# Softmax sums in 16 matmuls a step instead of 32, with the halves of each sum added by VectorE, and one side unit moved ahead of the second scores

## Chip, cores and metric

The kernel runs on one core of a Trainium2 chip. The metric is the device time of one execution in microseconds (us). Before the change the median of three runs is 751.95 us (751.55 to 753.9).

## What is computed

Two branches over the same 2048 x 512 input x are mixed by a gate. Branch A is a recurrent attention with memory: the sequence is cut into 64 segments of 32 tokens, each segment attends to itself and to 8 memory tokens, and the first 8 rows of a segment's output are the memory of the next. Branch B is a layer norm with a two-layer MLP. Cut to what matters here:

```
for s in range(64):                                  # 64 segments, in order
    h = concat([mem, x[s*32:(s+1)*32]])              # 8 + 32 rows
    q, k, v = h @ Wq, h @ Wk, h @ Wv                 # 32 heads of 128
    scores = where(mask, q @ k.T * scale, -1e9)
    p = softmax(scores)                              # exp / sum of exp
    o = (p @ v) @ Wo
    mem = o[:8]                                      # needed by the next segment
    outs.append(o[8:])
out = g * concat(outs) + (1 - g) * mlp(layernorm(x)) # g = sigmoid(sum(x * gate_w))
```

Because the memory is carried, a segment can't begin before the memory rows of the one ahead are known.

## The kernel before, in words

A first part of some 80 us loads all weights into SBUF and runs most of the MLP. Then a Python loop writes out 64 steps, one per segment. The order of the instructions on every engine is the order of the program text; nothing is rescheduled.

**Packing.** A step works on 32 columns at once: the 8 memory rows and 24 of the 32 tokens; the other 8 tokens of a segment ("left") have had their projections made ahead, four segments at a time. TensorE runs mostly in four strips of 32 columns (`tile_position=(0, 32 * j)`), so four matmuls in a row work side by side and a group of four is the unit to count. The 32 heads stand as 8 groups (i) of 4 (j); the first four groups are half 0, the others half 1. Each half has its own PSUM bank of scores, `SbF` for half 0 and `U[0]` for half 1, 56 columns a group.

**A step, in TensorE's order.** Four projections of queries and keys (`qk_unit`, L128, into `U`), each cast by ScalarE (L133) and transposed by VectorE (L137). Then `scores(s, 0)` (L266 and L270), whose exponentials ScalarE writes to the tile `E` (L805). Five V units (`v_unit`, L147). The sums for half 0. `scores(s, 1)`, whose exponentials come in two pieces (L794): columns 40 to 55, which belong to the memory queries, first, then columns 0 to 39. Two V units, a side unit, the memory sums of half 1, the last V unit. Two units of other work, a side unit, the side sums of half 1. Then the attention product `av` (L290 with V, L295 with VP; half 0 first, then half 1), and the output projection (L159), whose memory rows go through `new_mem` (L746, cast by VectorE in L748) into the next step's input.

**Two kinds of sums.** The sums for the memory queries (`msum`, L796) are needed at once: `mnorm` takes their reciprocal on VectorE (L801) and multiplies the columns 40 to 55 of `E` by it (L802) before `av` reads them. `sums` (L273) makes them in two rows of four matmuls, main part (L277) and left part (L280), which add up in PSUM. The sums for the other 32 queries (`xsums`, L697) can come later, since their product is divided afterwards: L701 makes them with the exponentials as the stationary operand, in two rows of four again, into 8 columns `xs8` of `SbF`. `recip_x` takes their reciprocal (L712), sends it to DRAM (`r_dr`, L715) and back, broadcast to all partitions, as `Rb` (L718), on SP's DMA queue, with the loads of `hm` (L646) between. In the next step POOL multiplies by it (`x_norm`, L730).

**Side units.** `next(mlp)` issues four matmuls of 256 columns (L674) of the MLP that was put off for some tiles. They wait for nothing in the step and are put at places by hand. `racc` (L722) and `rmin` (L865) collect the reciprocals for a range test at the end; `mask_put` (L259) writes the mask, and zeros for the sums, into `SbF` or `U[0]`.

Of the kernel before, what the change touches and what calls it, by code (L numbers as in the profile page):

```python
# [28 lines left out]
def kernel(ctx, tc, A_x, A_mem0, A_Wq, A_Wk, A_Wv, A_Wo, A_seg_len, B_x, B_w1, B_b1, B_w2, B_b2, gate_w, out):  # L29
    nc = tc.nc  # L30
    P = 128
    _, S, Dm = A_x.shape
    H, Dh = A_Wq.shape[1], A_Wq.shape[2]
    M = A_mem0.shape[1]
# [10 lines left out]
    NG = H // 4  # L45
    NP = H // 2
    EW = 56
    RIDE = 32 - M
    LEFT = seg - RIDE
# [8 lines left out]
    dram = ctx.enter_context(tc.tile_pool(name="dram", bufs=1, space=DRAM))  # L58
# [22 lines left out]
    MkF = ep.tile([P, 4 * EW + NG + 2 * M], BF16)  # L81
# [169 lines left out]


    RS = ep.tile([P, 32], FP32)
    RP = [SbF[:, 288:320], RS[:]]


    def mask_put(i2):
        c = 4 * EW + (NG + 2 * M if i2 == 0 else 0)
        nc.vector.tensor_copy(out=(SbF, U[0])[i2][:, 0:c], in_=MkF[:, 0:c])  # L259

    def scores(s, i2):
        T, si = divmod(s, SPT)
        for i in range(4 * i2, 4 * i2 + 4):
            for j in range(4):
                h = 4 * i + j
                nc.tensor.matmul(Sb[i2][32 * j:32 * j + 32, i - 4 * i2, M:M + 40], lhsT=KT[:, h // 2, :, h % 2], rhs=QT[:, h // 2, :, h % 2],  # L266
                                 start=False, stop=True, skip_group_check=True, tile_position=(0, 32 * j))
        for j in range(4):
            a0 = 8 * i2 + j // 2
            nc.tensor.matmul(Sb[i2][32 * j:32 * j + 32].rearrange("p i (a b) -> p i a b", b=8)[:, :, 0:7:6, :],  # L270
                             lhsT=KL[T % 2][:, si, j // 2, i2].rearrange("p l a b -> p (l a) b")[:, :, j % 2],
                             rhs=QT[:, a0:a0 + 7:2, :, j % 2].rearrange("p a (x q) -> p a x q", q=8)[:, :, 0:5:4, :],
                             start=False, stop=True, skip_group_check=True, tile_position=(0, 32 * j))  # L273

    def sums(out, E, c_main, c_left, n, start):
        for j in range(4):
            nc.tensor.matmul(out[32 * j:32 * j + 32], lhsT=BO[:, 32 * j:32 * j + 32], rhs=E[:, :, c_main:c_main + n],  # L277
                             start=start, stop=False, skip_group_check=True, tile_position=(0, 32 * j))
        for j in range(4):
            nc.tensor.matmul(out[32 * j:32 * j + 32, :, 0:8], lhsT=BO[:, 32 * j:32 * j + 32], rhs=E[:, :, c_left:c_left + 8],  # L280
                             start=False, stop=True, skip_group_check=True, tile_position=(0, 32 * j))
# [315 lines left out]
    racc = lp.tile([P, NG * 40], FP32)  # L597
    rmin = lp.tile([P, NG * 40], FP32)
    tot = lp.tile([P, 4], FP32)
    good = lp.tile([P, 2], BF16)  # L600
# [89 lines left out]
    mlp = mlp_halves()  # L690
    XRs, Rbs = {}, {}

    xs8 = SbF[:, 4 * EW:4 * EW + NG]
    xs8z = SbF[:, 4 * EW + NG:4 * EW + NG + 2 * M]
    RW = 9 * NG

    def xsums(E, h):  # L697

        for c0, n in ((8, 32), (0, LEFT)):
            for c in range(4):  # L700
                nc.tensor.matmul(xs8[32 * c:32 * c + n, 4 * h:4 * h + 4], lhsT=E[:, 4 * h + c, c0:c0 + n], rhs=BO[:, 0:P:32],  # L701
                                 start=False, stop=True, skip_group_check=True, tile_position=(0, 32 * c))

    def x_raw(s):
        XR = cx.tile([P, 4, NG, 32], BF16, tag="XR", name="XR")
# [3 lines left out]

    def recip_x(s):  # L710
        R = Rs.pop(s)
        nc.vector.reciprocal(out=R[:, 8 * NG:RW], in_=xs8)  # L712

        Rb = cw.tile([P, P, NG], FP32, tag="Rb", bufs=1, name="Rb")
        nc.sync.dma_start(r_dr[s % 2][:], R[:, 8 * NG:RW])  # L715
        hm_load(owed[0])
        owed[0] = 0
        nc.sync.dma_start(Rb[:].rearrange("p r e -> p (r e)"), r_dr[s % 2][:].rearrange("r e -> (r e)").partition_broadcast(P))  # L718
        for i2 in (1, 0):
            nc.vector.tensor_copy(out=R[:, 32 * i2:32 * i2 + 32], in_=RP[i2])  # L720
        mask_put(0)
        nc.gpsimd.tensor_tensor(out=racc[:, 0:RW], in0=racc[:, 0:RW], in1=R[:, 0:RW], op=ALU.add)  # L722
        Rbs[s] = Rb

    def x_norm(s):
        T, si = divmod(s, SPT)
        XR, Rb = XRs.pop(s), Rbs.pop(s)[:].rearrange("p (c q) (h j) -> p h j c q", c=4, h=2)
        for out, o, a, b in ((UT[(s + 1) % 2], M, LEFT, 32), (UL[T % 2], LEFT * si, 0, LEFT)):
            for h in range(2):
                nc.gpsimd.tensor_tensor(out=out[:, :, 4 * h:4 * h + 4, o:o + b - a], in0=XR[:, :, 4 * h:4 * h + 4, a:b], in1=Rb[:, h, :, :, a:b], op=ALU.mult)  # L730

    def wo_pass(U_, cuts=(0, Dm), bk=W):
        for n in range(NW):
# [19 lines left out]
    for s in range(nseg):  # L753
        T, si = divmod(s, SPT)
# [6 lines left out]
        if s >= 1:  # L761
            x_norm(s - 1)
# [24 lines left out]
        E = cx.tile([P, NG, EW], BF16, tag="E", name="E")  # L787
        R = cx.tile([P, NG * 40], FP32, tag="R", name="R")
# [5 lines left out]
            nc.scalar.activation(out=E[:, 4 * i2:4 * i2 + 4, c], in_=Sb[i2][:, :, c], func=ACTF.Exp, scale=scale)  # L794

        def msum(i2):  # L796
            sums(U[1 + 2 * i2][:, 320:352].rearrange("p (i q) -> p i q", q=8), E[:, 4 * i2:4 * i2 + 4, :], 40, 48, 8, True)

        def mnorm(i2):
            r, e = RP[i2], E[:, 4 * i2:4 * i2 + 4, 40:56].rearrange("p i (a q) -> p i a q", q=8)  # L800
            nc.vector.reciprocal(out=r, in_=U[1 + 2 * i2][:, 320:352])  # L801
            nc.vector.tensor_tensor(out=e, in0=e, in1=r.rearrange("p (i q) -> p i q", q=8).unsqueeze(2).to_broadcast([P, 4, 2, 8]), op=ALU.mult)  # L802

        scores(s, 0)
# [94 lines left out]
    wl, c = wls.pop(T), cs.pop(T)  # L899
    o = cw.tile([P, Dm], BF16, tag="o", bufs=1, name="o")  # L900
# [159 lines left out]
```

## Time and profile before

| | us |
|---|---|
| median of three runs | 751.95 |
| the profiled execution | 755.67 |
| its span, first to last instruction | 753.8 |
| TensorE busy | 736.0 (98%) |
| ScalarE busy | 535.6 (71%) |
| VectorE busy | 399.5 (53%) |
| POOL busy | 274.2 (36%) |

The profile is of one execution. A row of a timeline gives the start in us from the span's start, the busy time, the engine, the line of the program, the operation, the tiles out<-in, their sizes and how many instructions are merged in it; in square brackets stands how long the engine was idle before and what ended that. A row of a group by shape has busy time, mean ns of one instruction, and idle time ahead. PE is TensorE's matmul, PEld its weight load, DVE VectorE, ACT ScalarE. The row of a stretch has its length, and for each engine the busy time and the number of instructions, then the granted clock. Matmuls are pipelined and their ends are modelled, so their starts are what to read.

### The profile page before, as it was taken

The numbers are of one execution on the slowest core, as the hardware profiler recorded it, in microseconds if no ns is written. First come the engines' busy times: TensorE is split into PE (matmuls) and PEld (weight loads), VectorE is DVE, ScalarE is ACT, GpSimd is POOL, SyncE is SP. The second block draws the span as 40 slices with busy tenths as digits, with TensorE's granted clock in tenths as the row PEclk, the third lists the DMA queues.
The fourth block names the chain that finished last, engine by engine and source line by source line (L and its number), as shares of the span: only waits on it lengthen the run. The fifth ranks groups of instructions, "written<-read, shape, count | busy, mean of one in ns | idle before, by whom it ended". The sixth has DMA issues, their size and how long they took to land.

```text
span 753.8 us, 45384 instructions
## 1 busy us (share of the span) xinstructions
PE 736.0 (98%) x19896; PEld 429.8 (57%) x19896; DVE 399.5 (53%) x1415; ACT 535.6 (71%) x1627; POOL 274.2 (36%) x516
## 2 busy tenths in 40 slices
PE   8999999999999999999999999999999999999996
PEld 5776555555555555555555565555555655555553
DVE  6776555446454554445554545445464545555444
ACT  5777667777776776777777777767777777777663
POOL 4001323444324444334433344333443334433341
PEclk9999999999999999999999999999999999999999
DMA  9999323122321323221322313231323222222321
GB/s 312 343 335 362 104 85 87 55 76 72 93 77 46 91 70 96 69 83 53 92 77 80 86 46 93 68 96 67 70 72 86 79 72 78 57 90 74 95 70 37
DMA packets 69997, 77.17 MB, mean 102 GB/s; under 512 B 34873, under 2 KB 59938, under 8 KB 68258
## 3 DMA queue, kind: packets, MB, share of 16 engines
q1 hardware_dynamic: 68802, 72.65, 31.4%
q8 instruction: 157, 2.57, 1.4%
q0 software_dynamic: 448, 1.05, 0.5%
q10 hardware_dynamic: 544, 0.52, 0.3%
q14 instruction: 46, 0.38, 0.2%
HBM read 60.21 MB, written 7.70 MB: 90 GB/s over the span
## 4 chain that ended last, share of the span: by engine, by line
PE 91%; DVE 3%; DMA 2%; issue 2%; ACT 1%; POOL 0%; DVEq 0%; SPq 0%; ACTq 0%; POOLq 0%
PE U L128 33%; PE X L159 19%; PE X L147 17%; PE X L128 4%; PE U L290 3%; PE W L674 3%; PE U L147 2%; PE SbF L482 1%; PE U L266 1%; DMA xt<-in_A_x_dram 1%; PE W L482 1%; PE U L489 1%; DVE junk L465 1%; PE SbF L266 1%; PE SbF L701 1%
## 5 line engine op out<-in xcount | busy, mean ns | idle before, releaser
L730 POOL TENSOR_TENSOR UT<-XR,Rb 128x384 bf16<-128x384 bf16 x126 | 140.2, 1134 | 310.1 <-DMA Rb<-r_dr 252.6
L133 ACT CAST Tb<-U 128x512 bf16<-128x512 f32 x288 | 168.7, 586 | 78.7 <-PE U L128 72.5
L128 PEld LDWEIGHTS <-hT 128*32 128x32 bf16 x4096 | 108.9, 96 | 95.5 <-DVE hT L748 1.1
L147 PE MATMUL X<-Wv_sb,hT 128*32 128x512 bf16 x2048 | 144.9, 378 | 0.9 <-issue 0.9
L128 PE MATMUL U<-Wq_sb,hT 128*32 128x512 bf16 x2048 | 145.1, 380 | 0.0
L128 PE MATMUL U<-Wk_sb,hT 128*32 128x512 bf16 x2048 | 144.6, 379 | 0.0
L159 PE MATMUL X<-Wo_sb,UT 128*32 128x512 bf16 x2016 | 123.0, 380 | 0.2
L748 DVE CAST hT<-U 128x8 bf16<-128x8 f32 x126 | 21.0, 167 | 172.0 <-PE U L746 131.1
L811 ACT CAST V<-X 128x256 bf16<-128x256 f32 x256 | 88.7, 372 | 16.4 <-PE X L147 3.5
L137 DVE STREAM_TRANSPOSE QT<-Tb 128x256 f32<-128x256 f32 x128 | 57.0, 446 | 71.9 <-ACT Tb L133 71.5
L159 PEld LDWEIGHTS <-UT 128*32 128x32 bf16 x2048 | 56.6, 96 | 57.1 <-issue 17.7
L707 ACT CAST XR<-U 128x256 bf16<-128x256 f32 x252 | 78.6, 438 | 0.0
L737 ACT CAST w<-X 128x128 bf16<-128x128 f32 x189 | 44.8, 310 | 45.8 <-PE X L159 45.1
L137 DVE STREAM_TRANSPOSE KT<-Tb 128x256 f32<-128x256 f32 x128 | 57.0, 445 | 25.3 <-ACT Tb L133 25.3
L730 POOL TENSOR_TENSOR UL<-XR,Rb 128x128 bf16<-128x128 bf16 x126 | 60.2, 500 | 0.0
L147 PEld LDWEIGHTS <-hT 128*32 128x32 bf16 x2048 | 47.0, 94 | 22.3 <-issue 1.8
L842 ACT CAST UT<-U 128x64 bf16<-128x64 f32 x252 | 35.3, 227 | 28.2 <-PE U L295 28.2
L722 POOL TENSOR_TENSOR racc<-racc,R 128x72 f32<-128x72 f32 x63 | 21.2, 337 | 93.6 <-DVE R L720 49.9
L674 PE MATMUL W<-w_sb,hm 128*32 128x256 bf16 x728 | 52.7, 273 | 0.1
L794 ACT ACTIVATE E<-U 128x64 bf16<-128x64 f32 (+1 forms) x128 | 35.0, 273 | 11.3 <-PE U L270 11.1
L482 PEld LDWEIGHTS <-w_sb 128*128 128x128 bf16 (+1 forms) x352 | 33.5, 100 | 13.4 <-issue 2.4
L159 PE MATMUL X<-Wo_sb,UL 128*32 128x512 bf16 x512 | 39.8, 379 | 0.2 <-issue 0.2
(178 smaller groups left out, 1223.0 us busy)
## 6 DMA issues: line engine op xcount, KB each, us to landing
Rb<-r_dr SPq DMA_DIRECT2D x63, 512.0 KB, 3.9
Wv_sb<-in_A_Wv_dram SPq DMA_DIRECT2D x4, 1024.0 KB, 7.2
Wq_sb<-in_A_Wq_dram SPq DMA_DIRECT2D x4, 1024.0 KB, 8.5
Wk_sb<-in_A_Wk_dram SPq DMA_DIRECT2D x4, 1024.0 KB, 9.0
Wo_sb<-in_A_Wo_dram SPq DMA_DIRECT2D x4, 1024.0 KB, 9.7
VP<-VL SPq DMA_DIRECT2D x64, 64.0 KB, 3.2
hm<-h_dr SPq DMA_DIRECT2D x91, 32.0 KB, 2.2
c<-c_dr SPq DMA_DIRECT2D x16, 128.0 KB, 3.5
```

Of the source, the lines that this page charges most:

```text
L128: nc.tensor.matmul(bk[32 * j:32 * j + 32, :], lhsT=G[:, kc, :], rhs=W5[t][:, kc, h0:h1, j, :], start=(kc == 0), stop=(kc == KC - 1), tile_ ...
L133: nc.scalar.copy(out=Tb[:], in_=bk.rearrange("p (a b e) -> p a e b", a=8, b=2))
L137: nc.vector.transpose(out=dst[:, 8 * hf:8 * hf + 8, c0:c0 + 32, :].rearrange("p a r b -> p a (r b)").bitcast(FP32), in_=Tb[:].rearrange("p ...
L147: nc.tensor.matmul(bk[32 * j:32 * j + 32, :], lhsT=G[:, kc, :], rhs=Wv5[:, kc, 4 * vb:4 * vb + 4, j, :], start=(kc == 0), stop=(kc == KC - ...
L159: nc.tensor.matmul(bk[32 * c:32 * c + 32, :], lhsT=U_[:, j, i, :], rhs=Wo_sb[:, 4 * i + j, :], start=(n == 0), stop=(n == NW - 1), tile_po ...
L482: nc.tensor.matmul(hp[:rows, 0:TB * P], lhsT=w1_sb[:, kc, fc * P:fc * P + rows], rhs=yTs[blk][:, kc, :], start=(kc == 0), stop=(kc == KC - 1))
L674: nc.tensor.matmul(W[32 * c:32 * c + 32, cc], lhsT=hm[:, 32 * c:32 * c + 32], rhs=w2_sb[:, fc, cc], start=(fc == 0 and h == 0), stop=(fc = ...
L707: nc.scalar.copy(out=XR[:, j], in_=U[j][:, 0:NG * 40].rearrange("p (i q) -> p i q", q=40)[:, :, 0:32])
L730: nc.gpsimd.tensor_tensor(out=out[:, :, 4 * h:4 * h + 4, o:o + b - a], in0=XR[:, :, 4 * h:4 * h + 4, a:b], in1=Rb[:, h, :, :, a:b], op=ALU ...
L737: nc.scalar.copy(out=w[:, a:b], in_=bk[:, a:b])
L811: nc.scalar.copy(out=V[:, i0:i0 + 2, :].rearrange("p i e -> p (i e)"), in_=(X1, X2)[vb][:, 256 * h:256 * h + 256])
L842: nc.scalar.copy(out=UT[s % 2][:, j, :, 0:M], in_=U[j][:, 0:NG * 40].rearrange("p (i q) -> p i q", q=40)[:, :, 32:40])
```

## The change

`xsums` takes the block of ones `BO` as the stationary operand and the exponentials as the moving one, four matmuls of 40 columns for a half instead of eight of 4: their left and main parts come out in separate columns. `msum` does the same with 64 columns, four matmuls instead of eight. VectorE then adds the two parts by a TENSOR_REDUCE, once in each `mnorm` and once in `recip_x`. A step so has 16 matmuls of sums instead of 32. The side sums now stand as 32 x 2 columns of 8 equal rows each, so the reciprocal, `racc`, `rmin` and the mask put are wider, and the write to `r_dr` takes every eighth partition: 16 rows of 256 bytes instead of 128 of 32. One `next(mlp)` moves from ahead of the second `msum` to ahead of the second scores (in all steps but the first, as before).

```diff
-    r_dr = [dram.tile([P, NG], FP32, name=f"r_dr{i}") for i in range(2)]
+    r_dr = [dram.tile([16, 8 * NG], FP32, name=f"r_dr{i}") for i in range(2)]
...
-    RP = [SbF[:, 288:320], RS[:]]
+    RP = [SbF[:, 336:368], RS[:]]
...
-        c = 4 * EW + (NG + 2 * M if i2 == 0 else 0)
+        c = 4 * EW + (2 * XQ + 2 * M if i2 == 0 else 0)
...
-    xs8 = SbF[:, 4 * EW:4 * EW + NG]
-    RW = 9 * NG
+    xs = SbF[:, 4 * EW:4 * EW + 2 * XQ].rearrange("p (h q) -> p h q", h=2)
+    RW = 16 * NG
     def xsums(E, h):
-        for c0, n in ((8, 32), (0, LEFT)):
-            for c in range(4):
-                nc.tensor.matmul(xs8[32 * c:32 * c + n, 4 * h:4 * h + 4], lhsT=E[:, 4 * h + c, c0:c0 + n], rhs=BO[:, 0:P:32],
-                                 start=False, stop=True, skip_group_check=True, tile_position=(0, 32 * c))
+        for c in range(4):
+            nc.tensor.matmul(xs[32 * c:32 * c + 32, h, 0:40], lhsT=BO[:, 0:P:4], rhs=E[:, 4 * h + c, 0:40],
+                             start=False, stop=True, skip_group_check=True, tile_position=(0, 32 * c))
     def recip_x(s):
         R = Rs.pop(s)
-        nc.vector.reciprocal(out=R[:, 8 * NG:RW], in_=xs8)
-        Rb = cw.tile([P, P, NG], FP32, tag="Rb", bufs=1, name="Rb")
-        nc.sync.dma_start(r_dr[s % 2][:], R[:, 8 * NG:RW])
+        nc.vector.tensor_reduce(out=xs[:, :, 40:48], in_=xs[:, :, 0:16].rearrange("p h (a q) -> p h q a", a=2), axis=AX.X, op=ALU.add)
+        nc.vector.reciprocal(out=R[:, 8 * NG:RW].rearrange("p (h q) -> p h q", h=2), in_=xs[:, :, 16:48])
+        Rb = cw.tile([P, 16, 8 * NG], FP32, tag="Rb", bufs=1, name="Rb")
+        nc.sync.dma_start(r_dr[s % 2][:], R[0:P:8, 8 * NG:RW])
...
         def msum(i2):
-            sums(U[1 + 2 * i2][:, 320:352].rearrange("p (i q) -> p i q", q=8), E[:, 4 * i2:4 * i2 + 4, :], 40, 48, 8, True)
+            for j in range(4):
+                nc.tensor.matmul(U[1 + 2 * i2][32 * j:32 * j + 32, 320:384], lhsT=BO[:, 32 * j:32 * j + 32], rhs=E[:, 4 * i2:4 * i2 + 4, 40:56],
+                                 start=True, stop=True, skip_group_check=True, tile_position=(0, 32 * j))
         def mnorm(i2):
             r, e = RP[i2], E[:, 4 * i2:4 * i2 + 4, 40:56].rearrange("p i (a q) -> p i a q", q=8)
-            nc.vector.reciprocal(out=r, in_=U[1 + 2 * i2][:, 320:352])
+            m = U[1 + 2 * i2][:, 320:384].rearrange("p (i a q) -> p i q a", i=4, a=2)
+            nc.vector.tensor_reduce(out=r.rearrange("p (i q) -> p i q", q=8), in_=m, axis=AX.X, op=ALU.add)
+            nc.vector.reciprocal(out=r, in_=r)
...
             xsums(E, 0)
             msum(0)
             mnorm(0)
+            if s:
+                next(mlp, None)
         scores(s, 1)
...
         if not last:
-            if s:
-                next(mlp, None)
             msum(1)
             mnorm(1)
```

The order of TensorE's instructions around the second scores, before the change. `U_119` is the bank of half 0's memory sums, `U_118` that of half 1's scores.

```order
L280 LDWEIGHTS BO
L280 MATMUL U_119<-E,BO 32x32
L266 LDWEIGHTS KT
L266 MATMUL U_118<-QT,KT 32x40
L266 LDWEIGHTS KT
```

And the same place after it (lines of the changed kernel are one to five higher; L799 are the memory sums, L675 is the side unit, L267 the scores):

```order
L799 LDWEIGHTS BO
L799 MATMUL U_119<-E,BO 32x64
L675 LDWEIGHTS hm
L675 MATMUL W<-w_sb,hm 32x256
L675 LDWEIGHTS hm
L675 MATMUL W<-w_sb,hm 32x256
L675 LDWEIGHTS hm
L675 MATMUL W<-w_sb,hm 32x256
L675 LDWEIGHTS hm
L675 MATMUL W<-w_sb,hm 32x256
L267 LDWEIGHTS KT
L267 MATMUL U_118<-QT,KT 32x40
```

The side unit now stands between the sums of half 0 and the scores of half 1. Where it stood before, TensorE has these rows, from the V unit ahead to the memory sums of half 1 (`U_121`):

```order
L147 MATMUL X_123<-Wv_sb,hT_86 32x512
L674 LDWEIGHTS hm
L674 MATMUL W<-w_sb,hm 32x256
L674 LDWEIGHTS hm
L674 MATMUL W<-w_sb,hm 32x256
L674 LDWEIGHTS hm
L674 MATMUL W<-w_sb,hm 32x256
L674 LDWEIGHTS hm
L674 MATMUL W<-w_sb,hm 32x256
L277 LDWEIGHTS BO
L277 MATMUL U_121<-E,BO 32x32
```

After the change the memory sums follow the V unit directly:

```order
L148 MATMUL X_123<-Wv_sb,hT_86 32x512
L799 LDWEIGHTS BO
L799 MATMUL U_121<-E,BO 32x64
L799 LDWEIGHTS BO
L799 MATMUL U_121<-E,BO 32x64
```

On VectorE, from the first normalisation to the mask put, before:

```order
L801 RECIPROCAL SbF<-U_119 128x32
L802 TENSOR_TENSOR E<-E,SbF 128x4x16
L801 RECIPROCAL RS<-U_121 128x32
L802 TENSOR_TENSOR E<-E,RS 128x4x16
L712 RECIPROCAL R<-SbF 128x8
L720 COPY R<-RS 128x32
L720 COPY R<-SbF 128x32
L259 CAST SbF<-MkF 128x248
```

And after:

```order
L805 TENSOR_REDUCE SbF<-U_119 128x32
L806 RECIPROCAL SbF<-SbF 128x32
L807 TENSOR_TENSOR E<-E,SbF 128x4x16
L805 TENSOR_REDUCE RS<-U_121 128x32
L806 RECIPROCAL RS<-RS 128x32
L807 TENSOR_TENSOR E<-E,RS 128x4x16
L712 TENSOR_REDUCE SbF<-SbF 128x2x8
L713 RECIPROCAL R<-SbF 128x64
L721 COPY R<-RS 128x32
L721 COPY R<-SbF 128x32
L260 CAST SbF<-MkF 128x336
```

Three instructions more stand there in every step, one ahead of each reciprocal.

More of the change, by code (lines that the diff above doesn't have):

```diff
@@ L79 @@
     VP = [ep.tile([P, SPT, 2, Dh], BF16, name=f"VP{i}") for i in range(2)]
-    MkF = ep.tile([P, 4 * EW + NG + 2 * M], BF16)
+    XQ = 48
+    MkF = ep.tile([P, 4 * EW + 2 * XQ + 2 * M], BF16)
     Mk = MkF[:, 0:4 * EW].rearrange("p (a c) -> p a c", c=EW)
@@ L596 @@
     UL = [cw.tile([P, 4, NG, 32], BF16, tag=f"UL{i}", bufs=1, name=f"UL{i}") for i in range(2)]
-    racc = lp.tile([P, NG * 40], FP32)
+    racc = lp.tile([P, 16 * NG], FP32)
     rmin = lp.tile([P, NG * 40], FP32)
@@ L691 @@
     XRs, Rbs = {}, {}
-    xs8 = SbF[:, 4 * EW:4 * EW + NG]
-    xs8z = SbF[:, 4 * EW + NG:4 * EW + NG + 2 * M]
-    RW = 9 * NG
+    xs = SbF[:, 4 * EW:4 * EW + 2 * XQ].rearrange("p (h q) -> p h q", h=2)
+    xs8z = SbF[:, 4 * EW + 2 * XQ:4 * EW + 2 * XQ + 2 * M]
+    RW = 16 * NG
     def xsums(E, h):
-        for c0, n in ((8, 32), (0, LEFT)):
-            for c in range(4):
-                nc.tensor.matmul(xs8[32 * c:32 * c + n, 4 * h:4 * h + 4], lhsT=E[:, 4 * h + c, c0:c0 + n], rhs=BO[:, 0:P:32],
-                                 start=False, stop=True, skip_group_check=True, tile_position=(0, 32 * c))
+        for c in range(4):
+            nc.tensor.matmul(xs[32 * c:32 * c + 32, h, 0:40], lhsT=BO[:, 0:P:4], rhs=E[:, 4 * h + c, 0:40],
+                             start=False, stop=True, skip_group_check=True, tile_position=(0, 32 * c))
     def x_raw(s):
@@ L726, in x_norm @@
         T, si = divmod(s, SPT)
-        XR, Rb = XRs.pop(s), Rbs.pop(s)[:].rearrange("p (c q) (h j) -> p h j c q", c=4, h=2)
-        for out, o, a, b in ((UT[(s + 1) % 2], M, LEFT, 32), (UL[T % 2], LEFT * si, 0, LEFT)):
+        XR, Rb = XRs.pop(s), Rbs.pop(s)[:].rearrange("p (c j) (h q) -> p h j c q", c=4, h=2)
+        for out, o, a, b, r in ((UT[(s + 1) % 2], M, LEFT, 32, 0), (UL[T % 2], LEFT * si, 0, LEFT, 32 - LEFT)):
             for h in range(2):
-                nc.gpsimd.tensor_tensor(out=out[:, :, 4 * h:4 * h + 4, o:o + b - a], in0=XR[:, :, 4 * h:4 * h + 4, a:b], in1=Rb[:, h, :, :, a:b], op=ALU.mult)
+                nc.gpsimd.tensor_tensor(out=out[:, :, 4 * h:4 * h + 4, o:o + b - a], in0=XR[:, :, 4 * h:4 * h + 4, a:b], in1=Rb[:, h, :, :, r:r + b - a], op=ALU.mult)
     def wo_pass(U_, cuts=(0, Dm), bk=W):
```

## Prediction, written before the result was known

> **What bounds the kernel now.** I read the busy table first, then a timeline of one undisturbed step, then the wait table.
>
> ```profile
> PE 736.0 (98%) x19896; PEld 429.8 (57%) x19896; DVE 399.5 (53%) x1415; ACT 535.6 (71%) x1627; POOL 274.2 (36%) x516
> PEclk9999999999999999999999999999999999999999
> ```
>
> TensorE is busy 98% of the span at full granted clock. It is the engine whose order sets the time, and any other engine matters only where TensorE stops for it. So I look for what TensorE waits for in the stretch that the change touches. This is the timeline of the step whose first scores begin at 445.28 us.
>
> ```profile
> 446.12 0.45 DVE L137 STREAM_TRANSPOSE KT<-Tb 128x256 f32<-128x256 f32 x1 [0.42 <-ACT Tb L133]
> 446.49 0.20 PE L701 MATMUL SbF<-BO,E 128*32 128x4 bf16 x8
> 446.55 0.18 PE L277 MATMUL U<-E,BO 128*32 128x32 bf16 x4
> 446.57 0.18 PE L280 MATMUL U<-E,BO 128*32 128x32 bf16 x4
> 446.62 0.28 PE L266 MATMUL U<-QT,KT 128*32 128x40 bf16 x16
> 446.77 0.61 PE L147 MATMUL X<-Wv_sb,hT 128*32 128x512 bf16 x8
> 446.91 0.37 DVE L801 RECIPROCAL SbF<-U 128x32 f32<-128x32 f32 x1 [0.34 <-ACT V L811]
> 447.04 0.22 ACT L794 ACTIVATE E<-U 128x64 bf16<-128x64 f32 x1 [0.17 <-PE U L270]
> 447.20 0.29 PE L674 MATMUL W<-w_sb,hm 128*32 128x256 bf16 x4
> 447.31 0.22 DVE L802 TENSOR_TENSOR E<-E,SbF 128x64 bf16<-128x64 bf16 x1
> 447.32 0.20 PE L277 MATMUL U<-E,BO 128*32 128x32 bf16 x4
> 447.34 0.20 PE L280 MATMUL U<-E,BO 128*32 128x32 bf16 x4
> 447.37 0.40 PE L147 MATMUL X<-Wv_sb,hT 128*32 128x512 bf16 x4
> 447.60 0.36 DVE L801 RECIPROCAL RS<-U 128x32 f32<-128x32 f32 x1
> 447.81 0.65 ACT L811 CAST V<-X 128x256 bf16<-128x256 f32 x2
> 448.01 0.29 PE L674 MATMUL W<-w_sb,hm 128*32 128x256 bf16 x4
> 448.06 0.23 DVE L802 TENSOR_TENSOR E<-E,RS 128x64 bf16<-128x64 bf16 x1
> 448.12 0.22 PE L701 MATMUL SbF<-BO,E 128*32 128x4 bf16 x8
> 448.42 0.33 PE L290 MATMUL U<-E,V 32*128 32x40 bf16 x16
> 448.58 0.20 PE L295 MATMUL U<-E,VP 32*128 32x64 bf16 x4
> ```
>
> Read starts against starts, since a matmul's shown length is mostly pipeline. Four small matmuls on four column strips cost TensorE about 0.025 us (446.55 to 446.57), whether they are 4 or 32 columns wide. Three chains run close beside it. K's second transpose ends at 446.57, and the second scores start at 446.62. The second half's exponentials start 0.42 us after those scores, and the second sums start 0.28 us after the exponentials (447.32). Finally the second half of the attention product (L290, 448.42) needs E normalised by L802, which ends at 448.29: some 0.08 us of slack are left after a handover of 0.05.
>
> **TensorE's side of the change.** Every step loses four rows of four sums (two L701, one L277, one L280), 4 x 0.025 = 0.10 us or 6.3 us over 63 steps if nothing waited. But the chains take it back. In the clock of this step: one row of side sums at 446.49 and one row of main and left sums at 446.515, then the side unit, 0.11 us (448.01 to 448.12), so the second scores start at 446.65 instead of 446.62. K is ready by then; the side unit hides the wait for its transpose. Without the side unit there, the scores would still start at 446.62. The exponentials follow at 447.07 and the second sums at 447.35, 0.03 later than now. The two V units ahead of them end at 446.65 + 0.15 + 0.43 = 447.23, so TensorE stands for 0.12 us where the side unit used to be. One row of sums less, and the last V unit starts at 447.375 against 447.37. Nothing is gained up to there. Behind it the casts of V by ScalarE are where they were; one row fewer in the second L701 moves the attention product 0.03 us forward. TensorE's side alone is worth 0 to 0.10 us a step; I take 0.03, and the next part swallows even that.
>
> **VectorE's side: the term that decides.** Each normalisation gets a TENSOR_REDUCE (64 columns of PSUM to 32) ahead of its reciprocal. No such instruction runs on PSUM before; the nearest rows, from the groups by shape:
>
> ```profile
> L871 DVE TENSOR_REDUCE tot<-racc 128x1 f32<-128x320 f32 x1 | 0.5, 474 | 0.0
> L884 DVE TENSOR_REDUCE tot<-R 128x1 f32<-128x256 f32 x1 | 0.4, 414 | 0.0
> L720 DVE COPY R<-SbF 128x32 f32<-128x32 f32 x63 | 11.6, 183 | 0.1
> L801 DVE RECIPROCAL RS<-U 128x32 f32<-128x32 f32 x63 | 22.5, 358 | 5.5 <-PE U L280 0.5
> L712 DVE RECIPROCAL R<-SbF 128x8 f32<-128x8 f32 x63 | 13.0, 206 | 10.6 <-PE SbF L701 9.9 <-PE U L295 0.5
> ```
>
> The reduces cost 60 ns for 64 columns and about 0.15 us beside that, so 0.21; a 32-column copy out of PSUM is 0.18. I take 0.22 us, bounds 0.17 and 0.30 (strided pairs at half rate). The reciprocals stay at 0.36. First half: the reduce starts at 446.86 (0.34 after its sums, as now), ends 447.08, reciprocal to 447.48, product to 447.73. Second half: its sums would let the reduce start at 447.61, but it is queued behind that product on VectorE and starts near 447.65 (an independent instruction starts some 0.08 before the one ahead ends: L720 after L712). Reduce to 447.87, reciprocal to 448.26, 0.10 to the product as now (447.96 to 448.06), product to 448.59, matmul 0.05 later at 448.64. That is 0.22 behind today's 448.42. Some of it is already lost today: the second half now stops once more for V (the casts end at 448.46), which will be over by then. So the end of the product moves from 448.58 to about 448.74, **0.16 to 0.18 us a step**.
>
> The trace holds this very delay once by accident. In the step that starts at 361.99 L802 takes 0.53 us instead of 0.23, as POOL is at work in SBUF:
>
> ```profile
> 364.74 0.93 POOL L730 TENSOR_TENSOR UL<-XR,Rb 128x128 bf16<-128x128 bf16 x2
> 364.77 0.53 DVE L802 TENSOR_TENSOR E<-E,RS 128x64 bf16<-128x64 bf16 x1
> 365.36 0.28 PE L290 MATMUL U<-E,V 32*128 32x40 bf16 x16
> 445.28:455.45 10.17, 10.17 (x304) 5.73 (x300) 4.62 (x18) 7.67 (x24) 2.74 (x8) 1.00 0.28 82
> 361.99:372.36 10.37, 10.30 (x305) 5.75 (x300) 5.08 (x18) 7.68 (x24) 4.69 (x9) 1.00 0.25 82
> ```
>
> E is ready 3.31 us into that step (I expect 448.59 - 445.28 = 3.31 too), and the step takes 10.37 instead of 10.17 us. So the delay is not made up later. I take 0.18: 63 x 0.18 = **+11.3 us**. Bounds by the reduce's: 0.10 to 0.33, +6 to +21 us. [...] No run so far shows such a reduce.
>
> **What is free.** The reciprocal for the side sums grows from 8 to 64 columns: by 6.3 ns a column (L712 against L801) 0.56 us, with its own reduce, and with the mask put of 336 columns, some 1.0 us more of VectorE after the product.
>
> ```profile
> 451.77 0.42 DVE L748 CAST hT<-U 128x8 bf16<-128x8 f32 x2 [2.46 <-PE U L746]
> 366.07 0.40 PE L159 MATMUL X<-Wo_sb,UT 128*32 128x512 bf16 x4
> ```
>
> VectorE idles 2.46 us before its next work that TensorE waits for, the casts of the new memory (451.77); that hides it, and uncovered it would cost the 1.0. The reciprocals leave for DRAM about 0.7 us later, in 16 pieces instead of 128, and the hm loads and Rb behind them on SP's queue shift too. Rb serves POOL's L730, whose UT part the output projection needs: even in the late case at 361.99 UT is done at 364.74 and needed at 366.07, 1.3 us on. racc and rmin (72 to 128 columns, under 0.15 us each) sit in the same gaps.
>
> **What comes back.** Some steps hold a pause of TensorE that no engine explains:
>
> ```profile
> PEld L290 <- issue: 5.5, 12, 1.1
> PEld L147 <- issue: 3.1, 6, 1.2
> 293.03 0.40 PE L128 MATMUL X<-Wq_sb,GL 128*32 128x512 bf16 x4 [0.77 <-issue]
> 501.67 0.22 PE L290 MATMUL U<-E,V 32*128 32x40 bf16 x6 [1.00 <-issue]
> q8 instruction: 157, 2.57, 1.4%
> ```
>
> 157 packets of 16.4 KB for 39,792 TensorE records are 253 records a packet, and the pauses sit in or right behind the burst of small matmuls. I read them as waits for the next piece of program: 8 to 9 us in all (the two rows and a few smaller ones, less waits like that at 361.99). 32 of about 600 instructions a step (304 and 300 in the row of the stretch) go, all from the burst, and the new wait gives the fetch time. Bounds 0 to -9 us; I take -5.5, between the ends, since where the pieces' borders fall decides. [...]
>
> **Sum.** The profiled execution took 755.67 us with a span of 753.8; the median of the runs shown is 751.95, 3.7 lower. 755.67 + 11.3 - 5.5 = 761.5, less 3.7: **757.7 us**, 0.8% slower.
>
> **Rivals.**
> - *The burst gets faster (faster than before).* If the reduce costs its lower bound and starts without queueing, the delay is 0.10 us a step, +6.3, and all pauses go, -9: 749. If E comes in time as well, because VectorE overlaps the reduces with its neighbours more than L712 and L720 show, only the 0.03 and the pauses are left: 751.95 - 1.9 - 9 = 741. It decides at E ready by 448.37, 3.09 us into the step. For it: VectorE is at 53%. Against it: three instructions in each half that need one another, the second half's queued behind the first's.
> - *POOL in the way (slower still).* The reciprocal and product of the second half now read SBUF later, while L730, waiting on a later Rb, works later too. If every fourth more step meets it at 0.3 us as at 361.99: +5, 763; with the reduce at its upper bound 770.
> - *No pause goes.* The program's pieces fall as badly as now: 763.
> - *The change does not act:* the side unit merely trades places, and the waits move with it; this needs E on time and pauses unchanged: 751 to 752.
>
> **Chances.** Forecast with partial return of pauses (752 to 762) 0.48; pauses unchanged 0.12; POOL in the way 0.13; faster burst 0.19; no effect 0.08. I call a difference of 0.3% (2.3 us) the least that can be told from none. Same is the last case and the edges of the forecast (0.08) and of the faster burst (0.02), 0.18 together; faster 0.17; slower 0.65. The range 743 to 767 leaves out the far ends of the faster burst and of the POOL case.
>
> **What would show it.** After the change: the second L290 of a step starts about 3.36 us after its first scores, with a wait for VectorE's product; TENSOR_REDUCE near 0.22 us; second sums waiting for ScalarE's exponentials; fewer "issue" pauses. I am wrong if L290 starts at 3.1 as now, or if the reduce is under 0.15 us.

## The result and the profile after the change

The changed kernel takes 757.51 us (median of six runs, 755.93 to 757.66); the kernel before took 751.75 us beside it (six runs, 749.87 to 753.9). The ratio is 1.0075, 95% interval 1.0055 to 1.0095. The profiled execution took 757.62 us with a span of 755.8.

The busy table and the row of the program's own DMA queue, of the profile after:

```profile
PE 738.8 (98%) x18888; PEld 418.4 (55%) x18888; DVE 456.6 (60%) x1604; ACT 536.0 (71%) x1627; POOL 247.5 (33%) x516
...
q8 instruction: 149, 2.44, 1.3%
```

TensorE has 1,008 matmuls less (16 in each of 63 steps), and is busy as long as before (738.8 us against 736.0). VectorE has gained 57 us. This is the timeline of an undisturbed step after the change, the one that starts at 446.84 us; it stands against the step at 445.28 that the prediction showed of before.

```profile
448.05 0.19 PE L701 MATMUL SbF<-E,BO 128*32 128x40 bf16 x4
448.08 0.20 PE L799 MATMUL U<-E,BO 128*32 128x64 bf16 x4
448.11 0.28 PE L675 MATMUL W<-w_sb,hm 128*32 128x256 bf16 x4
448.22 0.27 PE L267 MATMUL U<-QT,KT 128*32 128x40 bf16 x16
448.35 0.61 PE L148 MATMUL X<-Wv_sb,hT 128*32 128x512 bf16 x8
448.40 0.23 DVE L805 TENSOR_REDUCE SbF<-U 128x32 f32<-128x64 f32 x1 [0.27 <-PE U L799]
448.61 0.23 ACT L795 ACTIVATE E<-U 128x64 bf16<-128x64 f32 x1 [0.17 <-PE U L271]
448.67 0.37 DVE L806 RECIPROCAL SbF<-SbF 128x32 f32<-128x32 f32 x1
448.88 0.21 PE L799 MATMUL U<-E,BO 128*32 128x64 bf16 x4
448.91 0.40 PE L148 MATMUL X<-Wv_sb,hT 128*32 128x512 bf16 x4
449.07 0.22 DVE L807 TENSOR_TENSOR E<-E,SbF 128x64 bf16<-128x64 bf16 x1
449.21 0.22 DVE L805 TENSOR_REDUCE RS<-U 128x32 f32<-128x64 f32 x1
449.46 0.36 DVE L806 RECIPROCAL RS<-RS 128x32 f32<-128x32 f32 x1
449.82 0.27 PE L291 MATMUL U<-E,V 32*128 32x40 bf16 x16
449.92 0.23 DVE L807 TENSOR_TENSOR E<-E,RS 128x64 bf16<-128x64 bf16 x1
450.20 0.28 PE L291 MATMUL U<-E,V 32*128 32x40 bf16 x16
```

Follow the second half. Its sums (L799) start at 448.88, its reduce at 449.21 behind the first half's product, its product ends at 450.15, and the second L291 starts at 450.20. That is 3.36 us into the step, against 3.14 before (448.42 in the step at 445.28). The first L291 started at 449.82; between the two, TensorE stands. The wait table says so too (total us, number, largest):

```profile
PEld L799 <- issue: 15.0, 63, 0.3
PEld L291 <- issue: 9.8, 44, 0.5
...
PE U L291 <- DVE E L807: 2.8, 12, 0.4
```

In this profile a matmul whose data is late shows up mostly on its weight load and as "issue"; only 12 of these waits are put down to VectorE's product by name. The 44 waits of 0.22 us on average at L291 are read as the late E, then, and not as pauses: in the step shown the matmuls start 0.05 us after the product ends. The 63 at L799 are the second sums waiting for ScalarE's exponentials (448.61 to 448.84 in this step, the sums at 448.88).

The step in one row of the stretch table is 10.35 us long; it was 10.17 to 10.18.

```profile
446.84:457.19 10.35, 10.28 (x288) 5.63 (x284) 5.58 (x21) 7.67 (x24) 3.13 (x8) 1.00 0.25 78
446.84:450.21 3.37, 3.30 (x132) 1.97 (x125) 2.48 (x9) 2.56 (x8) 1.82 (x4) 1.00 0.02 5
```

Over 63 steps, 0.17 us each is +10.7 us. Yet the two profiled executions differ by 2.0 us only. Add up what each step takes beyond a clean step of its kind: 13.2 us before, 4.4 us after. So 8.8 us of pauses went, and 10.7 - 8.8 = 1.9. In the medians the gap is 5.8, since the profiled execution of before lay 3.9 us above its median and that of after 0.1: without the profiler, before seems to lose some 4 us less in pauses than its profile shows (this is worked out, not seen).

### The profile page after: what moved, and what is told of

It reads as the page before. It is cut to its first block, busy times and chain, and to the rows that moved or that the text cites. A ratio compares the mean times of both kernels' runs of the same rounds, so it can differ in the third digit from the quotient of the medians.

```text
span 755.8 us, 43556 instructions
## 1 busy us (share of the span) xinstructions
PE 738.8 (98%) x18888; PEld 418.4 (55%) x18888; DVE 456.6 (60%) x1604; ACT 536.0 (71%) x1627; POOL 247.5 (33%) x516
## 5 line engine op out<-in xcount | busy, mean ns | idle before, releaser
L731 POOL TENSOR_TENSOR UT<-XR,Rb 128x384 bf16<-128x384 bf16 x126 | 114.2, 928 | 320.5 <-DMA Rb<-r_dr 229.5
L129 PEld LDWEIGHTS <-hT 128*32 128x32 bf16 x4096 | 107.2, 96 | 97.3 <-DVE hT L749 1.0
L148 PE MATMUL X<-Wv_sb,hT 128*32 128x512 bf16 x2048 | 142.6, 378 | 0.0
L160 PE MATMUL X<-Wo_sb,UT 128*32 128x512 bf16 x2016 | 120.4, 380 | 0.0
L723 POOL TENSOR_TENSOR racc<-racc,R 128x128 f32<-128x128 f32 x63 | 28.8, 457 | 113.4 <-DVE R L721 108.7
L148 PEld LDWEIGHTS <-hT 128*32 128x32 bf16 x2048 | 45.2, 95 | 20.8
L675 PE MATMUL W<-w_sb,hm 128*32 128x256 bf16 x728 | 51.2, 272 | 1.3 <-DMA hm<-h_dr 1.2
L731 POOL TENSOR_TENSOR UL<-XR,Rb 128x128 bf16<-128x128 bf16 x126 | 51.7, 433 | 0.0
L795 ACT ACTIVATE E<-U 128x64 bf16<-128x64 f32 (+1 forms) x128 | 35.0, 273 | 12.2 <-PE U L271 6.1
L291 PE MATMUL U<-E,V 32*128 32x40 bf16 x2048 | 35.2, 177 | 5.4 <-DVE E L807 2.8
```

What stands on the lines that cost most here:

```text
L129: nc.tensor.matmul(bk[32 * j:32 * j + 32, :], lhsT=G[:, kc, :], rhs=W5[t][:, kc, h0:h1, j, :], start=(kc == 0), stop=(kc == KC - 1), tile_ ...
L148: nc.tensor.matmul(bk[32 * j:32 * j + 32, :], lhsT=G[:, kc, :], rhs=Wv5[:, kc, 4 * vb:4 * vb + 4, j, :], start=(kc == 0), stop=(kc == KC - ...
L160: nc.tensor.matmul(bk[32 * c:32 * c + 32, :], lhsT=U_[:, j, i, :], rhs=Wo_sb[:, 4 * i + j, :], start=(n == 0), stop=(n == NW - 1), tile_po ...
L291: nc.tensor.matmul(Uv[j][:, i, :], lhsT=V[q, i, :], rhs=E[q, i, 8:48], start=(i == 0), stop=False, skip_group_check=True, tile_position=(3 ...
L675: nc.tensor.matmul(W[32 * c:32 * c + 32, cc], lhsT=hm[:, 32 * c:32 * c + 32], rhs=w2_sb[:, fc, cc], start=(fc == 0 and h == 0), stop=(fc = ...
```

## The experiments

**Theory E**: the two reduces lengthen VectorE's chain in front of the second half of the attention product, and this alone makes the step longer. **Rival S**: it is the side unit's move, which leaves the second sums waiting for ScalarE. **Rival Q**: it is the queue on VectorE, where the first half's reduce pushes everything behind it back. For the pauses there were three ideas: they went because the program is shorter in the dense stretch (P), because the new wait gives the loading time (W), or because of where the borders of the program's blocks happen to fall (B). The runs were made on three chips, on which the kernel before took 752.05, 755.07 and 755.27 us; so ratios are compared, and clean steps, which don't depend on pauses. The forecasts in us were made for a kernel before of 751.75; a ratio times this number is what to hold against them.

**1. The change without the side unit's move.** Against the kernel after:

```diff
             mnorm(0)
-            if s:
-                next(mlp, None)
         scores(s, 1)
...
         if not last:
+            if s:
+                next(mlp, None)
             msum(1)
```

> All of the change but the side unit, which stands ahead of the second memory sums again. Theory E (VectorE's longer chain to the second half of the attention product is the whole cost): that chain is queued behind the first half's product on VectorE, so it ends 3.30 us into a step whether the scores start at 1.34 or 1.37; second L291 still at 3.35, a step 10.35, time as the changed kernel, 756 to 758.5. Rival S (the wait of 0.24 us a step that opened at the memory sums, where the side unit was taken away, is the cost): that wait goes, a step near 10.2, 748 to 752.

758.43 us, ratio 1.0086 (1.0067 to 1.0105), clean step 10.34 to 10.38. The whole loss is still there, so Rival S falls.

**2. The side unit's move alone**: the reverse edit, on the kernel before.

> The kernel before with the side unit moved ahead of the second scores, and nothing else. Theory E: with four rows of sums ahead of it the scores start at 1.42 instead of 1.34, so everything behind moves by about 0.08 us a step, 5 us, less at most 3 us of pauses: 753 to 757, with the second L290 near 3.22. Rival S: the wait opens at the memory sums here too and the cost is that of the whole change, 0.17 a step, 757 or more. A third, that the side unit hides K's transpose and gains: under 751.

754.93 us, ratio 1.0039 (1.0021 to 1.0058), clean step 10.22 to 10.27. By itself the move costs 0.05 to 0.07 us a step, since the second sums now wait:

```profile
PEld L277 <- issue: 15.6, 64, 0.5
```

In the whole change this costs nothing, as E is later still.

**3. The side sums alone**: on the kernel before, one row of four matmuls in xsums, recip_x with its reduce, and the compact reciprocals through DRAM; memory sums and side unit as before.

> Only the side sums in the new form (8 matmuls fewer a step, their parts added off the path); memory sums, their normalisation and the side unit as before. Theory E: the chain to the second half of the attention product is untouched, so a step without pauses stays at 10.17 to 10.20 (the row saved ends in the wait for V); 16 instructions fewer and POOL's multiplication no longer strided take some of the pauses and of POOL's interference: 746 to 751. Rival (every row saved on TensorE counts): 0.05 us a step more, 743 to 747. Rival (the longer reciprocal in recip_x and the later Rb cost something): 753 or more.

750.62 us, ratio 0.9984 (0.9966 to 1.0002), clean step 10.15 to 10.20. Free, as forecast, and no gain that can be told from none.

**4. The memory sums alone**: on the kernel before, only msum and mnorm in their new form.

> Only the memory sums in the new form with the reduces on VectorE; side sums and side unit as before. Theory E: the first half's reduce starts 0.03 later than in the changed kernel (two rows of side sums ahead), so E is ready at 3.32 and the second L290 at 3.38; a step 10.38, time 757 to 762. Rival S: the side unit still fills its place, so near 752.

758.47 us, ratio 1.0093 (1.0073 to 1.0113), clean step 10.37 to 10.41. Two rows of the step that starts at 447.13 in that run: E is ready at 3.34 us, the second product of attention starts at 3.38.

```profile
450.24 0.23 DVE L806 TENSOR_TENSOR E<-E,RS 128x64 bf16<-128x64 bf16 x1
450.51 0.28 PE L290 MATMUL U<-E,V 32*128 32x40 bf16 x16
```

This one part holds the whole loss.

**5 and 6. Which of the two reduces?** On the kernel after, one half gets its old sums back:

```diff
...
+        def msum(i2):
+            (msum_o if i2 == 1 else msum_n)(i2)
+
+        def mnorm(i2):
+            (mnorm_o if i2 == 1 else mnorm_n)(i2)
```

(with `i2 == 0` in the other run; `_o` is the form before, `_n` the form after).

> The kernel after the change, with only the second half's memory sums and normalisation in their old form (two rows of four sums, no reduce on VectorE); the first half keeps its reduce. Theory E (each half's own reduce lengthens the chain in front of the second half of the attention product, and only the second half's counts): the second half's product ends 3.05 to 3.08 us into a step, the second L290 group starts at 3.10 to 3.15 as before the change, a clean step takes 10.17 to 10.22 us, and the time is 748 to 752 us. Rival Q (the queue on VectorE: it is the first half's reduce that pushes everything behind it back): the second half's product still ends after 3.2 us, a clean step takes 10.28 or more, and the time is 754 to 758 us.

755.14 us, ratio 1.0001 (0.9984 to 1.0019), clean step 10.17 to 10.22. The time in us is over its forecast since this chip runs the kernel before in 755.07; the ratio gives 751.8. In the step that starts at 497.70 E is ready at 500.74, 3.04 us in, and the second L291 follows without a stop:

```profile
500.06 0.35 DVE L814 RECIPROCAL RS<-U 128x32 f32<-128x32 f32 x1
500.51 0.23 DVE L815 TENSOR_TENSOR E<-E,RS 128x64 bf16<-128x64 bf16 x1
...
500.82 0.34 PE L291 MATMUL U<-E,V 32*128 32x40 bf16 x16
```

> The kernel after the change, with only the first half's memory sums and normalisation in their old form; the second half keeps its reduce. Theory E: the second half's own reduce (0.22 us) costs nearly all by itself, the queue behind the first half adds 0.01 to 0.03 us; the second half's product ends 3.26 to 3.30 us into a step, a clean step takes 10.31 to 10.36 us, and the time is 755 to 758 us. Rival Q: with the first half's reduce gone the second half is on time (product before 3.15 us), a clean step takes 10.17 to 10.24, and the time is 747 to 752 us.

761.44 us, ratio 1.0078 (1.0047 to 1.0110), clean step 10.31 to 10.37. Here too the time in us is over its forecast, and the ratio gives 757.6. In the step that starts at 503.45 E is ready 3.27 us in:

```profile
505.77 0.23 DVE L805 TENSOR_REDUCE RS<-U 128x32 f32<-128x64 f32 x1
506.03 0.35 DVE L806 RECIPROCAL RS<-RS 128x32 f32<-128x32 f32 x1
506.49 0.23 DVE L807 TENSOR_TENSOR E<-E,RS 128x64 bf16<-128x64 bf16 x1
506.77 0.28 PE L291 MATMUL U<-E,V 32*128 32x40 bf16 x16
```

So the first half's reduce adds 0.01 to 0.02 us to a step (the gap of half 1 old to before, and of half 0 old to after), and the second half's costs nearly everything. Theory E stands, Rival Q falls.

**7. As many instructions as before.** On the kernel after:

```diff
         if not last:
+            for _ in range(4):
+                for j in range(4):
+                    nc.tensor.matmul(U[3][32 * j:32 * j + 32, 384:416], lhsT=BO[:, 32 * j:32 * j + 32], rhs=BO[:, 0:32], ...)
             msum(1)
```

> The kernel after the change with 16 small matmuls a step (32 columns, into columns that nothing reads) put ahead of the second half's memory sums, where TensorE waits 0.12 us for ScalarE's exponentials: four groups of about 0.025 us, so the clean step should keep its 10.35 us within 0.03. It gives the program back the instructions that the change took out of it. Theory P (the pauses left because the program is shorter in the dense stretch): pauses of 0.8 to 1.2 us come back at some steps, and the time is 759 to 763 us. Rival W (they left because the new wait gives the program's loading time): no pauses come back, and the time is 757 to 759 us, by 0 to 2 us for the groups themselves.

766.03 us, ratio 1.0135 (1.0110 to 1.0160). The clean step keeps its 10.35 to 10.38 us, so the 16 matmuls fit into the wait for ScalarE; yet the ratio rises from 1.0075 to 1.0135, and pauses are back, this one at the very matmuls behind them:

```profile
549.05 0.10 PEld L799 LDWEIGHTS <-BO 128*32 128x32 bf16 x3 [0.90 <-issue]
549.05 0.21 PE L799 MATMUL U<-E,BO 128*32 128x64 bf16 x3 [0.76 <-issue]
```

The ratio gives 761.9 us, within the forecast of idea P. The step is as long as in the kernel after, and only the instructions are more. The padding fills the wait for ScalarE (at L799 2.0 us in 3 waits are left, of 15.0 in 63) but leaves the wait for E, which is still there in most steps (it was 9.8 us in 44 waits in the kernel after):

```profile
PEld L291 <- issue: 9.3, 41, 0.6
```

The other wait, for ScalarE, stands in run 2 in 64 places, and there, too, the pauses stay (21 borders in the table below). So idea W as it was put, that a wait as such removes the pauses, falls.

**8 and 9. The borders moved.** On the kernel before, and then on the kernel after:

```diff
-        warm(NWARM)
+        warm(NWARM - 8)
+        for _ in range(64):
+            nc.tensor.matmul(U[3][:, 0:64], lhsT=ident[:], rhs=ident[:, 0:64], ...)
```

> The kernel before the change with 8 of its warm-up matmuls at the start cut into 64 short ones of the same columns in all: 112 more TensorE records ahead of the main loop, nothing else changed. Theory B (the pauses sit at borders of equal blocks of the program, every 256 records of TensorE): their place modulo 256 moves from 194 to about 82, or for an unmoved count of records stays at another fixed place; they hit other lines than before, and the time moves by up to 4 us either way (748 to 756). Rival C (the pauses belong to certain lines of the step, such as the burst of small matmuls, whatever their number): the same lines and steps pause as before, and the time stays within 1 us of before.

758.37 us, ratio 1.0042 (1.0024 to 1.0059). I numbered TensorE's instructions (matmuls, weight loads and the semaphore instructions of its queue) in program order and matched them with the trace. In the kernel before, the pauses of over 0.45 us in the main loop, 293.03 and 501.67 among them, fall on instruction 194 or 195 modulo 256. With 112 instructions more ahead of the loop they still do, and so they come in other steps. The pause of 293.03 is in the step that starts at 288.35; the one most like it is now in the step that starts at 246.76, two matmuls earlier in the step:

```profile
251.35 0.61 PE L128 MATMUL X<-Wq_sb,GL 128*32 128x512 bf16 x6 [0.78 <-issue]
```

In the other profiles it is the same number again, where they have pauses of this size; longer stops elsewhere wait for data of another engine or of a DMA (in the kernel after up to 0.9 us at L747 for ScalarE's w, and up to 1.0 us at L675 for the load of hm). So the pauses are at borders of blocks of 256 instructions, and Rival C, that certain lines pause whatever their number, falls. What C has right is the place: in both kernels nearly all of these pauses stand between the attention product and the first matmuls of the output projection (before 11 of 12, all but the one at 89.96 us), in whichever steps a border falls there. The longer time says nothing of the borders: in the profiled executions the main loop takes 659.6 us, against 659.7 in the kernel before, and 2.2 us of the rise lie ahead of it, where the warm-up was cut up (80.2 us against 78.0). My forecast of a new remainder of about 82 was muddled: the remainder counts from the program's start, so it stays, and the instructions on it change.

> The kernel after the change, with the same 112 more TensorE records ahead of its main loop as in the run that moved the borders of the kernel before: the step is the same, only the borders of the blocks of 256 records fall on other instructions of it. Theory B (how much the pauses cost is decided by where the borders fall in the dense part of the step, and the changed kernel happens to have them well): the clean step stays at 10.35 us, pauses come back, ratio to before 1.011 to 1.020. Rival W (the changed step itself has no pauses, since its new wait gives the fetch time): ratio 1.005 to 1.010, as for the change itself.

761.59 us, ratio 1.0090 (1.0057 to 1.0123), clean step 10.35, six borders with a pause as in the kernel after. Idea B falls: the changed step has few pauses at both places of its borders.

**10 and 11. Sums without a reduce and with few instructions.** `BO` is block diagonal, so one full-width matmul does what four on column strips do. The first run has this edit on the kernel before, the second has the new side sums as well:

```diff
         def msum(i2):
-            sums(U[1 + 2 * i2][:, 320:352].rearrange("p (i q) -> p i q", q=8), E[:, 4 * i2:4 * i2 + 4, :], 40, 48, 8, True)
+            o, e = U[1 + 2 * i2][:, 320:352].rearrange("p (i q) -> p i q", q=8), E[:, 4 * i2:4 * i2 + 4, :]
+            nc.tensor.matmul(o, lhsT=BO[:], rhs=e[:, :, 40:48], start=True, stop=False, skip_group_check=True)
+            nc.tensor.matmul(o, lhsT=BO[:], rhs=e[:, :, 48:56], start=False, stop=True, skip_group_check=True)
```

> The kernel before the change, with the memory sums in full-width matmuls: the matrix of ones is block diagonal, so two matmuls of 128 columns of weights (main columns, then left columns into the same PSUM) give what eight matmuls on column strips give; 12 matmuls and 12 weight loads a step go, and VectorE's part is untouched. Theory E (what cost the change its time was VectorE's reduce in the chain, not TensorE's fewer matmuls): E is ready in time, the clean step stays at 10.13 to 10.22 us, and with fewer records in the dense part the ratio is 0.990 to 1.000. Rival: a full-width matmul has to wait for all four strips and for its 128-column weights, and costs 0.1 us or more beyond a group of four: clean step 10.3 to 10.6, ratio 1.01 to 1.03.

> The kernel before the change with the new side sums of the change (one row of four matmuls, the reduce off the path) and with the memory sums in full-width matmuls; the side unit in its old place. 20 matmuls a step go, and no reduce stands in front of the attention product. Theory E: clean step 10.10 to 10.20 us, ratio 0.985 to 0.999. Rival (full-width costs): clean step 10.3 to 10.6, ratio 1.01 to 1.03.

763.05 us, ratio 1.0114 (1.0087 to 1.0142), and 766.06 us, ratio 1.0150 (1.0122 to 1.0177). Both missed, and the rival's figures were right: the clean steps are 10.5 us. In the second of the two runs:

```profile
452.73 0.19 PE L701 MATMUL SbF<-E,BO 128*32 128x40 bf16 x4
...
452.85 0.19 PE L799 MATMUL U<-E,BO 128*128 128x32 bf16 x1
...
452.89 0.18 PE L800 MATMUL U<-E,BO 128*128 128x32 bf16 x1
453.00 0.28 PE L267 MATMUL U<-QT,KT 128*32 128x40 bf16 x16
```

From the side sums to the scores it takes 0.27 us from start to start (452.73 to 453.00), with two full-width matmuls between; two groups on strips and a whole side unit take 0.17 (448.05 to 448.22 after the change). The scores don't wait for K here: its transpose had ended at 452.81. The first full-width matmul is shown to start together with its weight load, 0.12 us after the group ahead (452.73 to 452.85); whether it is the four strips or the 128 columns of weights that it waits for is not shown.

**12. What the runs point to.** The kernel before with the new side sums, and the new memory sums in the first half alone, where the reduce is hidden; the side unit in its old place.

> The kernel before the change with the new side sums and, for the first half alone, the new memory sums with their reduce; second half and side unit as before. Theory E: the first half's reduce is hidden, the second half's product is at most 0.03 us later, the clean step is 10.15 to 10.20 us, ratio 0.993 to 1.002. Rival Q (the first half's reduce pushes the second half's chain back through VectorE's queue): clean step over 10.25, ratio 1.003 to 1.008.

751.98 us beside 755.27, ratio 0.9949 (0.9929 to 0.9970): it beats the kernel before, and by its ratio the kernel after. Its clean step is that of before within 0.02 us, at most 1.3 us over 63 steps, so most of the gain is not in the step:

```profile
446.47:456.62 10.15, 10.15 (x292) 5.72 (x288) 5.45 (x20) 7.67 (x24) 3.68 (x8) 1.00 0.19 55
```

Where the gain lies is not shown. Its profile has 3.1 us less pauses at borders than that of before, but as long a main loop (659.2 us against 659.7), since other stops took more; the profiled execution was the slowest of its twelve (755.21).

**What sets the pauses.** The runs were not planned for this count, but the 14 profiles allow it. For every matmul start of a clean step, take the time since the start of the matmul 128 ahead of it, which is 256 instructions with the weight loads; the table has the shortest such time, and the number of starts at which it is under 3.5 us (a bound chosen with the counts in view). Beside them: the borders with a pause of over 0.08 us, and their sum.

| kernel | clean step, us more than before | shortest 256, us | starts under 3.5 us | borders paused | us | ratio |
|---|---|---|---|---|---|---|
| before | 0 | 2.64 | 68 | 26 | 12.2 | 1 |
| before, borders moved (8) | 0 | 2.64 | 68 | 23 | 10.2 | 1.0042 |
| side unit moved (2) | 0.06 | 2.70 | 68 | 21 | 6.6 | 1.0039 |
| after, padded (7) | 0.18 | 2.81 | 64 | 27 | 10.3 | 1.0135 |
| side sums (3) | 0 | 3.06 | 60 | 20 | 6.2 | 0.9984 |
| best (12) | -0.02 | 3.10 | 53 | 23 | 9.1 | 0.9949 |
| half 1 old (5) | 0.01 | 3.12 | 48 | 20 | 7.6 | 1.0001 |
| half 0 old (6) | 0.15 | 3.31 | 48 | 21 | 8.5 | 1.0078 |
| memory sums (4) | 0.20 | 3.07 | 52 | 4 | 1.2 | 1.0093 |
| after, borders moved (9) | 0.17 | 3.37 | 20 | 6 | 1.8 | 1.0090 |
| sums without side unit (1) | 0.17 | 3.37 | 24 | 3 | 0.9 | 1.0086 |
| after | 0.17 | 3.37 | 20 | 6 | 0.8 | 1.0075 |
| full width, memory sums (10) | 0.34 | 3.48 | 8 | 2 | 0.6 | 1.0114 |
| full width, both (11) | 0.33 | 3.57 | 0 | 0 | 0.0 | 1.0150 |

Two rows show what is counted: the second row of the stretches after the change above (3.37 us, 132 matmuls and 125 weight loads), and the same of the kernel before:

```profile
446.06:448.71 2.65, 2.65 (x133) 1.80 (x125) 1.82 (x8) 2.01 (x8) 0.51 (x2) 1.00 0.00 0
```

In 13 of the 14 kernels the count goes with the pauses: with 48 dense starts or more, 20 or more borders pause; with 24 or fewer, at most 6. The memory sums alone break the rule, with 52 dense starts, a shortest time of 3.07 us and only 4 paused borders. Nor does it hold border by border. In steps 4 to 61 of the side sums alone and of the memory sums alone, 25 of 128 borders come at the end of 256 instructions done within 3.5 us; 5 and 2 of these pause, and in the side sums alone 12 others pause, behind 256 instructions that took 3.6 to 5.0 us. So a dense stretch as counted here does not by itself set a pause.

The program's packets look like a wait for the program but don't settle it: in the main loop of the kernel before, half of them land more than 2.3 us after a border was passed and a tenth more than 3.4 us after it, in the kernel after 2.1 and 2.9. The trace doesn't tell which block a packet holds. What is shown is that the pauses lie at the borders, and that 16 matmuls and their weight loads more in a step of the same length bring them back (run 7). Whether longer steps help as well stays open. The memory sums alone, with as many instructions as the side sums alone and a step longer by 0.20 us, have 4 paused borders against 20; but half 0 old, with 8 instructions less than these and a step longer by 0.15 us, has 21.

## Why the prediction was right, point by point

- *TensorE bounds, and its own saving is swallowed*: right. The second scores were put at 1.37 us into the step and start at 1.38 (448.22); the second sums at 2.07, found 2.04, behind a wait of about 0.1 (the V units ahead start at 448.35 and take 0.43). The side sums alone, 0.03 a step by that reasoning, gave no difference that can be told.
- *A reduce of 0.22 us, twice*: right, by the groups of the profile after.

```profile
L805 DVE TENSOR_REDUCE SbF<-U 128x32 f32<-128x64 f32 x63 | 14.6, 232 | 17.4 <-PE U L799 9.3 <-PE W L675 7.5 <-PE U L271 0.6
L805 DVE TENSOR_REDUCE RS<-U 128x32 f32<-128x64 f32 x63 | 13.6, 216 | 0.0
```

  Two of the nearest rows of the trace give a little more than was taken from them: 474 ns for 320 columns and 414 for 256 leave 0.17 us beside the columns, not 0.15, and so an estimate of 0.23 us for 64 columns. The half rate for strided pairs, behind the upper bound of 0.30, was a guess that no run shows: these two reduces add such pairs, in 232 and 216 ns.
- *E ready at 3.31 us, the second L290 at 3.36, +0.18 a step*: 3.31 and 3.36 in the step shown, and +0.17. The term was +11.3 and is +10.7. The accidental late step of the trace of before had told the size. That the second half's own reduce costs nearly all was not said in so many words; half 0 old showed it.
- *What is free*: right. The reciprocal of 64 columns takes 0.557 us and was put at 0.56. VectorE's idle time ahead of the casts of the new memory falls from 2.46 to 1.94 us, so there is room left. The first row is a group of the profile after, the second is from the timeline of its step at 446.84.

```profile
L713 DVE RECIPROCAL R<-SbF 128x64 f32<-128x64 f32 x63 | 35.1, 557 | 5.5
453.51 0.42 DVE L749 CAST hT<-U 128x8 bf16<-128x8 f32 x2 [1.94 <-PE U L747]
```

- *What comes back, -5.5 us*: the middle of a range from 0 to -9, and the medians give 5.8 - 10.7 = -4.9. In the profiles it was the far end, -8.8. The size was right partly by luck, as the profiled execution of before overstated its pauses. Of the reasons given, fewer instructions is borne out by the padded kernel (run 7). Time from the new wait is not enough by itself: that kernel has as long a step, and the pauses came back. Whether it helps is open. "Where the pieces' borders fall decides" is not borne out either (run 9).
- *Rivals*: the faster burst needed E by 3.09 us and found it at 3.31. POOL did not come in the way more than before: the second product takes 254 ns in the mean, and took 274 (before, the 49 of them beside which POOL did nothing took at most 226 ns, the 14 beside L730 up to 667). The rival that no pause goes fell, since most of them went. That the change does nothing was off: its parts act against each other.

## What to carry to other kernels

An instruction moved off the busiest engine is no gain if its replacement stands in a chain that this engine waits for: follow the chain to the matmul that needs its end, and price the one link that is added (here 0.22 us in front of a product with 0.08 us of slack). The same edit was free where the chain had room, in the first half and at the side sums, so split such a change by place before it is taken or dropped. And where "issue" pauses stand between instructions, compare clean steps and not only times: here fewer pauses gave back a part of the loss, and the time alone hid what the edit really costs.

## What the runs showed of the hardware

- In the kernel before, the pauses of TensorE of over 0.45 us that no engine and no DMA explains lay at borders of 256 of its instructions (number 194 or 195 modulo 256), 11 of 12 of them around the end of the attention product, and lasted up to 1.2 us.
- POOL's multiply of the side product got faster with a layout in which the reciprocals of its 128 x 384 operand lie side by side: 1134 ns before (in the memory sums alone two of them took 2.23 us, at 445.68), 926 in run 11, which has the new side sums, and after

```profile
L731 POOL TENSOR_TENSOR UT<-XR,Rb 128x384 bf16<-128x384 bf16 x126 | 114.2, 928 | 320.5 <-DMA Rb<-r_dr 229.5 <-ACT Tb L134 66.2 <-ACT E L810 24.8
```

- In run 11 a full-width matmul of 32 columns between groups on column strips starts 0.12 us after the group ahead (452.73 to 452.85), where in the kernel after strip groups follow each other at 0.03 us (448.05 to 448.08).
